# Batch 0 of a fused attention and gated FFN kernel: weight loads in 4 KB runs, conversion steps placed one by one, q turned by VectorE

## The chip, the cores and the metric

One core of a Trainium2 chip runs the whole program. The metric is the device time of one execution in microseconds; before the change it is 783.39 us, the median of three runs (782.16 to 783.68).

## What is computed

For each of 8 batches and 8 heads (S = 576 tokens, head size 64), 32 packed queries p attend to k and v, and then q attends to what came out, taken as keys and as values. The 4608 rows that result (8 heads side by side, 512 wide) go through a gated FFN. Cut to what matters:

```
pp  = softmax(p @ k.T / 8) @ v                  # per batch and head, 32 x 64
x   = softmax(q @ pp.T / 8) @ pp                # per batch and head, 576 x 64
x   = x.transpose(0, 2, 1, 3).reshape(4608, 512)
out = ((x @ w_a) * (x @ w_b)) @ w_out           # 512 x 1536, 512 x 1536, 1536 x 512
```

q, k, v and p are float32. The three weights come as float64, 6.29 MB each.

## The kernel before

**Stages of a batch.** Stage 1 (`stage1`, once for each half e of the heads) makes the scores of p against k, their softmax a1, its transpose and pp. Stage 2 (`stage2`, once for each half u of the tokens) makes the scores of q against pp and their softmax a2, which it stores as two float32r parts, `a2_hi` and `a2_lo`. x itself is never formed: `g_tiles` multiplies pp into a chunk c of the weights (128 columns of w_a and 128 of w_b for each of two f tiles), which gives `ghi` and `glo`, and `mm1` multiplies these by a2. So six chunks serve the twelve f tiles of a batch. An f tile of mm1 is two halves, one for w_a and one for w_b (`mm1_half`, 12 matmuls each, in a pair of PSUM banks of the pool `m`, of which there are two pairs). ScalarE copies the first half out, VectorE multiplies the second by it (both in `asb`), ScalarE rounds the product to `h_hi`, and GpSimd makes the rest `h_lo`. mm2 then adds up twelve f tiles against `wo` (hi and lo).

**Batch 0 and the weights.** The weights lie in DRAM as float64. Each piece of 512 KB is loaded raw into one of 12 buffers (`load_w`, `load_wout`) and turned to float32 by three steps: one on the high word (ScalarE, L170), one on the low word (ScalarE L176 or VectorE L173) and one that joins the words (VectorE, L178) into `w_ab`, or for w_out into `ob`, which is then split into `wo` hi (ScalarE) and lo (GpSimd). This happens once, while batch 0 runs; from batch 1 on the weights are in place. A chunk c needs four pieces: w_a and w_b, each for two pairs of heads. A piece of w_a or w_b is loaded by two DMAs, each to 64 of the 128 partitions, in runs of 2 KB. A piece of w_out is one DMA to 128 partitions, in runs of 4 KB.

**Order of the work.** It is written by hand; every engine takes its instructions in that order. `START` is the order of batch 0 up to the first f tile. In it K and Q are steps that turn k and q through TensorE (copies that bring two halves of the heads together, 18 transposes, copies out of PSUM), S0 and S1 begin stage 1, r0 and r1 go on with it, s0 and s1 are steps of stage 2, c is one round of up to three conversion steps, and g the first `g_tiles`. During mm1 and mm2 of a batch `between()` stands after every half f tile (slots 0 to 23) and after every f of mm2, and puts in what a table has for that slot: for batch 0 `PLAN_0`, which prepares batch 1 (Lp, Lk, Lv, Lq load; T0 turns p on TensorE; k0, k1, q0, q1 turn the two tiles of k or q on VectorE), and one round of conversions per slot. All loads go through SP's one DMA queue. At most eight DMAs are open; an issue beyond that waits for the eighth before it.

Of the kernel before, what the change touches and what calls it, by code (L numbers as in the profile page):

```python
# [19 lines left out]
def tile_packed_attn_gated_ffn(  # L20
# [144 lines left out]
    def to_f32(dst, raw, way):  # L165

        low, high = raw[..., 0], raw[..., 1].bitcast(F32)
        nc.scalar.activation(out=high, in_=high, func=AF.Prelu, scale=2.0 ** -112, alpha=-2.0 ** 32)  # L170
        yield
# [11 lines left out]
    def load_w(c, n):  # L183

        w, rr = (w_a, w_b)[n // 2], n % 2
        raw = wop.tile([P, 2, 2 * P, 2], U32, name="raw", tag="w")
        for e in range(E):
            row = (R * e + 2 * rr) * D
            nc.sync.dma_start(
                out=raw[D * e:D * e + D],  # L190
                in_=w.bitcast(U32)[row:row + 2 * D, 4 * P * c:4 * P * c + 4 * P].rearrange("(r d) f -> d r f", d=D))
        raws[c, n] = raw

    def load_wout(f):
# [3 lines left out]
        raws[NC, f] = raw  # L198

    wo_hi, wo_lo = [], []  # L200

    def convert(c, r):
        raw = raws.pop((c, r))
        if c < NC:
            i, rr = divmod(r, 2)
            yield from to_f32(lambda: w_ab[:, c, 2 * rr:2 * rr + 2, 2 * P * i:2 * P * i + 2 * P], raw, r == 3)
            return
        ts = []

        def dst():  # L210
            ts.append(sm.tile([P, DO], F32, name="ob", bufs=1))
            return ts[0]

        yield from to_f32(dst, raw, r % 3 == 2)
        t = ts[0]
# [15 lines left out]
    def stage1(b, e):  # L231

        rows = slice(64 * e, 64 * e + 64)
        s = bank_pair(True)
# [21 lines left out]
        tp, tq = bank(), bank()  # L256
# [19 lines left out]
    def stage2(b, u):  # L276

        TU = E * XH
        if b:
            hi, lo = (t[:, :, HS * u:HS * u + HS] for t in (a2_hi, a2_lo))  # L280
        else:
            hi, lo = (t.rearrange("p e (l x) -> p e x l", x=TX)[:, :, XH * u:XH * u + XH] for t in (a2_hi, a2_lo))
        x = bank_pair(True)
# [99 lines left out]
    def emit(b, plan, tasks={}):  # L383

        for name in plan.split():
            if name in tasks:
                next(tasks[name], None)
                continue
            what, e = name[:-1], int(name[-1])
# [52 lines left out]
    def converted(n):  # L442

        flight = []
        for _ in range(n):
            if not pieces:
                break
            if pieces[0] not in raws:
                load_pieces(1, True)
            flight.append(convert(*pieces.pop(0)))  # L450
            for c in flight[::-1]:
                next(c, None)
# [1 line left out]
            yield
            if len(flight) == 3:
                flight.pop(0)
        while flight:
            for c in flight[::-1]:
                next(c, None)
            yield  # L460
            if len(flight) == 1:
                drain(flight[0])
            flight.pop(0)
# [9 lines left out]
    q0 = scratch.tile([P, E, TX, D], F32, name="q0")
    for e in range(E):
        load_nat(k0[:, e].rearrange("p x d -> p (x d)"), k, 0, e)
    load_v(0, 0)
    for e in range(E):
        load_nat(q0[:, e].rearrange("p x d -> p (x d)"), q, 0, e)
    load_v(0, 1)
    load_pieces(8)  # L480
# [12 lines left out]
    for b in range(B):  # L493
        plan = dict(PLAN if b else PLAN_0)
        conv = converted(len(pieces))
        slot = [0]

        def between():
            emit(b + 1, plan.get(slot[0], "") if b + 1 < B else "")
            if b == 0:  # L500
# [13 lines left out]
        if b == 0:  # L514
# [57 lines left out]
```

## Time and profile before

| | |
|---|---|
| median of 3 runs | 783.39 us |
| the profiled execution's own time | 784.82 us |
| its span, first to last instruction | 783.0 us |
| TensorE matmul busy | 746.8 us (95%) |
| VectorE, ScalarE, GpSimd busy | 307.1, 288.1, 189.8 us |
| moved by DMA | 58.01 MB |
| mean granted TensorE clock | 0.974 |

The profiled execution took 784.82 us, of which 1.8 lie outside the span, and is 1.4 us above the median. The clock in the rows is a share of full speed, 1.00 or 0.50 in any short stretch; a mean over a longer stretch mixes the two. Times in rows are counted from the start of the span.

### The profile page before, as it was taken

How to read it: one execution, taken by the hardware profiler on the slowest of the kernel's cores; microseconds unless marked ns; L12 is line 12 of the kernel's file. 1: busy time of each engine (PE TensorE's matmuls, PEld its weight loads, DVE VectorE, ACT ScalarE, POOL GpSimd, SP SyncE). 2: the span in 40 equal slices, each digit the busy share in tenths (PEclk: the TensorE clock that was granted, in tenths of full speed). 3: DMA queues.
4: the chain of work that ended last, by engine and by line, in shares of the span. 5: the costliest groups of instructions: out<-in, count | busy, mean ns of one | idle time of the engine just before them, and what ended most of it. 6: DMA issues, size and time to landing. Idle time of an engine off the chain costs nothing.

```text
span 783.0 us, 13393 instructions
## 1 busy us (share of the span) xinstructions
PE 746.8 (95%) x5688; PEld 604.0 (77%) x5688; DVE 307.1 (39%) x487; ACT 288.1 (37%) x503; POOL 189.8 (24%) x146
## 2 busy tenths in 40 slices
PE   4667989999999999999999999999999999999998
PEld 2355677778887788788888788788877788888987
DVE  2756554555413445054421544144440444323200
ACT  2556774344312442144311443134411443134300
POOL 1012254323400234022410234012420224113300
PEclk8668999999999999999999999999999999999999
DMA  9999915145012340044201450142300410000001
GB/s 264 240 217 231 303 59 118 56 69 109 8 41 51 72 92 15 28 78 91 32 28 41 65 111 12 41 78 62 61 28 28 75 32 1 28 28 1 1 28 40
DMA packets 160459, 58.01 MB, mean 74 GB/s; under 512 B 139280, under 2 KB 147728, under 8 KB 160400
## 3 DMA queue, kind: packets, MB, share of 16 engines
q1 hardware_dynamic: 160400, 57.16, 31.4%
q8 instruction: 44, 0.72, 0.4%
q14 instruction: 15, 0.12, 0.1%
HBM read 47.71 MB, written 9.44 MB: 73 GB/s over the span
## 4 chain that ended last, share of the span: by engine, by line
PE 88%; DMA 4%; DVE 3%; ACT 2%; issue 1%; POOL 1%; SPq 0%; DVEq 0%; ACTq 0%; POOLq 0%
PE m L362 38%; PE m L340 38%; PE x L321 6%; PE s L237 2%; PE x L268 2%; DMA nat<-in_q_dram 1%; PE s L287 1%; DMA q<-in_q_dram 1%; PE x L258 1%; DMA raw<-in_moe_w_out_dram 1%; DMA raw<-in_moe_w_b_dram 1%; DVE w_ab L178 1%; POOL wo L83 0%; DVE ob L178 0%; ACT a_hi L309 0%
## 5 line engine op out<-in xcount | busy, mean ns | idle before, releaser
L362 PE MATMUL m<-wo,h_hi 128*128 128x512 f32 (+1 forms) x888 | 271.8, 388 | 3.2 <-ACT asb L348 2.0
L83 POOL TENSOR_TENSOR h_lo<-asb,h_hi 128x576 fp32r<-128x576 f32 x96 | 137.3, 1430 | 466.6 <-ACT h_hi L355 466.6
L362 PEld LDWEIGHTS m<-wo,h_hi 128*128 128x128 f32 x888 | 163.6, 189 | 47.6 <-ACT ob L375 7.5
L340 PE MATMUL m<-a_hi,ghi 128*128 128x288 f32 x768 | 175.5, 310 | 8.0 <-ACT a_hi L309 7.8
L362 PE MATMUL m<-wo,h_lo 128*128 128x512 f32 (+1 forms) x444 | 171.0, 385 | 0.0
L340 PE MATMUL m<-a_lo,ghi 128*128 128x288 f32 x768 | 164.9, 297 | 0.4 <-DVE a_lo L83 0.4
L340 PEld LDWEIGHTS m<-a_hi,ghi 128*128 128x128 f32 x768 | 122.7, 190 | 52.6 <-issue 37.6
L340 PE MATMUL m<-a_hi,glo 128*128 128x288 f32 x768 | 134.5, 297 | 0.0
L355 ACT CAST h_hi<-asb 128x576 fp32r<-128x576 f32 x96 | 64.8, 675 | 169.5 <-DVE asb L351 169.3
L340 PEld LDWEIGHTS m<-a_lo,ghi 128*128 128x128 f32 x768 | 125.6, 191 | 0.8 <-DVE a_lo L83 0.8
L351 DVE TENSOR_TENSOR asb<-m,asb 128x576 f32<-128x576 f32 x96 | 72.7, 757 | 131.9 <-PE m L340 124.6
L83 DVE TENSOR_TENSOR glo<-x,ghi 128x512 fp32r<-128x512 f32 x96 | 61.8, 685 | 141.5 <-ACT ghi L327 141.5
L340 PEld LDWEIGHTS m<-a_hi,glo 128*128 128x128 f32 x768 | 114.0, 191 | 0.0
L362 PEld LDWEIGHTS m<-wo,h_lo 128*128 128x128 f32 x444 | 83.9, 189 | 17.0
L375 ACT COPY ob<-m 128x512 f32<-128x512 f32 x35 | 20.6, 588 | 173.6 <-PE m L362 172.0
L348 ACT COPY asb<-m 128x576 f32<-128x576 f32 x96 | 61.5, 641 | 28.5 <-PE m L340 25.5
L321 PE MATMUL x<-w_ab,ppT 64*32 64x512 f32 x768 | 60.1, 615 | 7.5 <-DVE w_ab L178 7.5
L327 ACT CAST ghi<-x 128x512 fp32r<-128x512 f32 x96 | 51.3, 587 | 5.9 <-PE x L321 5.9
L118 DVE STREAM_TRANSPOSE xT<-nat 128x1152 f32<-128x1152 f32 x28 | 38.3, 1368 | 0.0
L321 PEld LDWEIGHTS x<-w_ab,ppT 64*32 64x32 f32 x768 | 9.5, 106 | 22.8 <-DVE w_ab L178 14.4
L170 ACT ACTIVATE raw<-raw 128x512 f32<-128x512 f32 x36 | 24.3, 677 | 3.0 <-DMA raw<-in_moe_w_out_dram 3.0
L298 ACT ACTIVATE t<-t 128x576 f32<-128x576 f32 x14 | 9.6, 687 | 42.8 <-POOL t L296 42.8
(91 smaller groups left out, 386.5 us busy)
## 6 DMA issues: line engine op xcount, KB each, us to landing
vt<-in_v_dram SPq DMA_DIRECT2D x16, 512.0 KB, 4.1
nat<-in_k_dram SPq DMA_DIRECT2D x56, 144.0 KB, 3.0
nat<-in_q_dram SPq DMA_DIRECT2D x56, 144.0 KB, 3.1
out_dram<-ob SPq DMA_DIRECT2D x31, 256.0 KB, 2.0
raw<-in_moe_w_a_dram SPq DMA_DIRECT2D x24, 256.0 KB, 8.7
raw<-in_moe_w_b_dram SPq DMA_DIRECT2D x24, 256.0 KB, 8.6
raw<-in_moe_w_out_dram SPq DMA_DIRECT2D x12, 512.0 KB, 6.7
out_dram<-ob SPq DMA_DIRECT2D x10, 128.0 KB, 2.3
```

The lines of the kernel that those rows point to most:

```text
L83: return eng.tensor_tensor(out=dst, in0=src, in1=hi.bitcast(F32), op=ALU.subtract)
L118: nc.vector.transpose(out=xT.rearrange("p r t -> p (r t)"), in_=t.rearrange("p r x d -> p (r x d)"))
L170: nc.scalar.activation(out=high, in_=high, func=AF.Prelu, scale=2.0 ** -112, alpha=-2.0 ** 32)
L237: nc.tensor.matmul(out=s[J * r:J * r + J, half, 0:HS], lhsT=pT[rows, r, :], rhs=xT_cols(b, "k", rows, r, half), start=True, stop=True)
L321: nc.tensor.matmul(out=gps[e][J * r:J * r + J, :], lhsT=ppT[rows, b % 2, r, :], rhs=w_ab[rows, c, r, :], start=True, stop=True)
L327: nc.scalar.copy(out=ghi[:, e], in_=gps[e])
L340: nc.tensor.matmul(out=ps[:, half, 0:HS], lhsT=gt[:, kt, i, :], rhs=at[:, kt, HS * half:HS * half + HS], start=(n == 0), stop=(n == len(st ...
L348: nc.scalar.copy(out=asb, in_=pa)
L351: nc.vector.tensor_tensor(out=asb, in0=pb, in1=asb, op=ALU.mult)
L355: nc.scalar.copy(out=hh, in_=flat)
L362: nc.tensor.matmul(out=o[:, cols], lhsT=ht[:, c0:c0 + P], rhs=wt[:, cols], start=(ft == 0 and n == 0), stop=(ft == NFT - 1 and n == 2))
L375: nc.scalar.copy(out=ob, in_=o)
```

## The change

It alters batch 0 alone, and the loads and conversions that run in it.

- A weight piece is now the 64 rows of one r for both halves of the heads and 512 float64 columns, so a run is 4 KB. It is still two DMAs to 64 partitions each. Eight pieces now serve two chunks at once (c = 0 and 1, then 2 and 3, then 4 and 5).
- The three conversion steps are letters of the tables, placed singly: A (high word, ScalarE), B (low word), C (join, VectorE) and D (split of w_out). B goes by `WAY`: of four pieces one to ScalarE, two to GpSimd, one to VectorE.
- q of batch 0 is loaded as in the other batches (eight DMAs in runs of 128 bytes) and turned by VectorE; its 18 transposes on TensorE and the copies around them go. The tokens of q then stand in their natural order, so a2 is written without a stride.
- The first loads come in another order (`FIRST`), and the loads for batch 1 stand elsewhere in `PLAN_0`.
- f tile 0 of batch 0 runs by halves of the tokens; stage 1 of e = 1 and stage 2 of u = 1 take their banks in batch 0 from the pool `m`.

The diff, cut to its core:

```diff
-                copy = nc.vector.tensor_copy if e else nc.gpsimd.tensor_copy if key == "q" else nc.scalar.copy
+                copy = nc.vector.tensor_copy if e else nc.scalar.copy
...
+    def low_word(raw, way):
+        low = raw[..., 0]
         if way:
-            nc.vector.tensor_scalar(
+            (nc.vector if way == 1 else nc.gpsimd).tensor_scalar(
                 out=low, in0=low, scalar1=2.0 ** -29, scalar2=7.0, op0=ALU.mult, op1=ALU.min)
...
-        w, rr = (w_a, w_b)[n // 2], n % 2
-        raw = wop.tile([P, 2, 2 * P, 2], U32, name="raw", tag="w")
+        w, r = (w_a, w_b)[n // R], n % R
+        raw = wop.tile([P, 4 * P, 2], U32, name="raw", tag="w")
         for e in range(E):
-            row = (R * e + 2 * rr) * D
+            row = (R * e + r) * D
             nc.sync.dma_start(
-                out=raw[D * e:D * e + D],
-                in_=w.bitcast(U32)[row:row + 2 * D, 4 * P * c:4 * P * c + 4 * P].rearrange("(r d) f -> d r f", d=D))
+                out=raw[D * e:D * e + D].rearrange("p f t -> p (f t)"),
+                in_=w.bitcast(U32)[row:row + D, 8 * P * c:8 * P * c + 8 * P])
...
+    WAY = (0, 2, 2, 1)
...
-        s = bank_pair(True)
+        s = bank_pair(b or e == 0)
...
+        if b == 0 and ft == 0:
+            pa, pb = (mm1_half(i, ghi, glo, halves=(0,)) for i in range(2))
+            mm1_half(0, ghi, glo, pa, (1,))
...
-    START = ("T0 K K K K Q K K K S0 Q S1 Q r0 r0 Q r1 Q r1 Q r0 Q c r1 P0 c c c s0 c s0 s1 s1 s0 c s0 s1 s1 g s0 s0 s1 s1 "
-             "c c c c")
+    FIRST = ("p0 k0 k1 w4 q0 v1 v0 q1 w8")
+    START = ("K K T0 B A K K K K K S0 A S1 C B A C r0 r0 r1 B C B r1 A A A r0 q0 r1 B A P0 q1 C s1 s1 A B s0 C C B "
+             "B s1 B B A s0 s1 s0 A A C C s0 g s0 B s1 s0 A A s1 A")
...
-    PLAN_0 = {0: "Lp0", 2: "Lk0", 4: "Lk1", 6: "Lv0", 8: "T0 k0", 9: "Lp2 k1 Lq0 Lq1", 15: "S0", 16: "r0",
-              19: "r0 S1", 20: "r0 r1 Lv1", 23: "r1", 24: "r1 Lv2", 25: "q0 P0", 26: "q1", 28: "Lk2", 29: "Lk3",
-              30: "s0", 31: "s0 s1", 32: "s0 s1", 33: "s0 s1", 34: "s1 s0 s0", 35: "s1", 36: "s1"}
-    NCONV = [1] * 24 + [1] * 12
+    PLAN_0 = ("B C C A | C C | B B A Lv0 B Lp0 B | Lk0 | A Lk1 C A C B B C C | B B C | B C A A B | T0 B | k0 A A C "
+              "A | C A B k1 | A C C B B A Lq1 Lq0 | B C | A C S0 |  |  | C D r0 A |  | C D | C D S1 | r0 | Lp2 B | "
+              "C r0 B r1 B | D A B A | Lv1 C B r1 B C | r1 D B | P0 Lv2 A | q0 C q1 B | A D C s0 A D D | A C s0 D "
+              "s1 A | D s0 Lk2 Lk3 |  | C s1 |  | s1 s1 | s0 D s0 s0 |  | C s1 s1")
```

**SP, the loads from the middle of the weights on, before.** `raw` is a weight piece, `nat` a tile of k (L109, first two) or q of batch 1, `vt` its v, `p_nat` its p:

```order
L189 DMA raw<-in_moe_w_b_dram 64x2x512 x4
L189 DMA raw<-in_moe_w_a_dram 64x2x512 x2
L133 DMA p_nat<-in_p_dram 128x2x64
L189 DMA raw<-in_moe_w_a_dram 64x2x512 x2
L189 DMA raw<-in_moe_w_b_dram 64x2x512 x2
L109 DMA nat_528<-in_k_dram 32x36x32 x4
L189 DMA raw<-in_moe_w_b_dram 64x2x512 x2
L189 DMA raw<-in_moe_w_a_dram 64x2x512 x2
L109 DMA nat_576<-in_k_dram 32x36x32 x4
L189 DMA raw<-in_moe_w_a_dram 64x2x512 x2
L189 DMA raw<-in_moe_w_b_dram 64x2x512 x2
L126 DMA vt<-in_v_dram 128x4x256
```

Now, from the first load of w_b:

```order
L194 DMA raw<-in_moe_w_b_dram 64x1024 x8
L194 DMA raw<-in_moe_w_a_dram 64x1024 x8
L194 DMA raw<-in_moe_w_b_dram 64x1024 x8
L194 DMA raw<-in_moe_w_a_dram 64x1024 x8
L194 DMA raw<-in_moe_w_b_dram 64x1024 x8
L127 DMA vt<-in_v_dram 128x4x256
L129 DMA vt<-in_v_dram 64x4x64
L134 DMA p_nat<-in_p_dram 128x2x64
L110 DMA nat_553<-in_k_dram 32x36x32 x4
L110 DMA nat_574<-in_k_dram 32x36x32 x4
L201 DMA raw<-in_moe_w_out_dram 128x1024 x10
```

Batch 1's p and k stood among the weight pieces and now stand behind all 24 of them.

**TensorE, around T0** (the matmul that reads `p_nat`), before, from the first half of f tile 3:

```order
L340 MATMUL m<-a_hi,ghi 128x288 x2
L340 MATMUL m<-a_lo,ghi 128x288 x2
L340 MATMUL m<-a_hi,glo 128x288 x4
L226 MATMUL x<-ident,p_nat 128x128
L340 MATMUL m<-a_hi,ghi 128x288 x2
L340 MATMUL m<-a_lo,ghi 128x288 x2
L340 MATMUL m<-a_hi,ghi 128x288 x2
L340 MATMUL m<-a_lo,ghi 128x288 x2
L340 MATMUL m<-a_hi,glo 128x288 x4
L321 MATMUL x<-w_ab,ppT 32x512 x8
```

Now:

```order
L335 MATMUL m<-a_hi,ghi 128x288 x2
L335 MATMUL m<-a_lo,ghi 128x288 x2
L335 MATMUL m<-a_hi,glo 128x288 x4
L220 MATMUL x<-ident,p_nat 128x128
L335 MATMUL m<-a_hi,ghi 128x288 x2
L335 MATMUL m<-a_lo,ghi 128x288 x2
L335 MATMUL m<-a_hi,ghi 128x288 x2
L335 MATMUL m<-a_lo,ghi 128x288 x2
L335 MATMUL m<-a_hi,glo 128x288 x4
L335 MATMUL m<-a_hi,ghi 128x288 x2
L335 MATMUL m<-a_lo,ghi 128x288 x2
```

T0 moved up by half an f tile (`PLAN_0` slot 8 to slot 7): it stood in f tile 4 and now stands ahead of it.

**VectorE, around T0's copy into `pT`**, before:

```order
L351 TENSOR_TENSOR asb<-m,asb 128x576
L178 SCALAR_TENSOR_TENSOR w_ab<-raw 128x2x256
L227 COPY pT<-x 128x128
L118 STREAM_TRANSPOSE xT_688<-nat_528 128x1152
L173 TENSOR_SCALAR raw<-raw 128x512
L178 SCALAR_TENSOR_TENSOR w_ab<-raw 128x2x256
L351 TENSOR_TENSOR asb<-m,asb 128x576
L118 STREAM_TRANSPOSE xT_713<-nat_576 128x1152
L178 SCALAR_TENSOR_TENSOR w_ab<-raw 128x2x256
L83 TENSOR_TENSOR glo<-x,ghi 128x512 x2
```

Now:

```order
L350 TENSOR_TENSOR asb<-m,asb 128x576
L221 COPY pT<-x 128x128
L119 STREAM_TRANSPOSE xT_688<-nat_553 128x1152
L182 SCALAR_TENSOR_TENSOR w_ab<-raw 128x2x256
L350 TENSOR_TENSOR asb<-m,asb 128x576
L182 SCALAR_TENSOR_TENSOR w_ab<-raw 128x2x256
L176 TENSOR_SCALAR raw<-raw 128x512
L119 STREAM_TRANSPOSE xT_717<-nat_574 128x1152
L84 TENSOR_TENSOR glo<-x,ghi 128x512 x2
L182 SCALAR_TENSOR_TENSOR w_ab<-raw 128x2x256 x2
L350 TENSOR_TENSOR asb<-m,asb 128x576
L182 SCALAR_TENSOR_TENSOR w_ab<-raw 128x2x256 x2
```

The order of the turns of k (L119) and of the multiplications `asb` behind them is much as it was, one f tile's multiplication behind each turn.

## Rows read from the trace of the kernel before

**Rows 1.** Stretches: us, length, busy of each engine (instructions), PEclk, DMA share, GB/s
```profile
5.00:10.00 5.00, 2.39 (x12) 2.42 (x13) 1.97 (x3) 1.92 (x4) 0.00 (x0) 1.00 1.04 355
10.00:15.00 5.00, 2.39 (x20) 1.61 (x22) 2.34 (x4) 0.76 (x2) 1.27 (x2) 0.95 1.09 283
15.00:40.00 25.00, 16.53 (x181) 7.38 (x173) 15.53 (x34) 13.12 (x25) 2.67 (x2) 0.64 1.07 240
75.00:80.00 5.00, 5.00 (x27) 4.05 (x20) 1.89 (x3) 1.78 (x4) 0.00 (x0) 0.56 1.05 295
80.00:85.00 5.00, 4.50 (x35) 4.04 (x38) 3.01 (x5) 3.98 (x7) 1.44 (x1) 1.00 0.98 156
90.00:95.00 5.00, 4.82 (x43) 3.72 (x41) 4.17 (x8) 3.73 (x9) 1.43 (x1) 1.00 1.02 411
...
200.00:300.00 100.00, 100.00 (x760) 82.33 (x758) 35.57 (x56) 32.17 (x56) 24.09 (x19) 1.00 0.23 50
```

**Rows 2.** TensorE's waits, the whole span: total us, times, longest
```profile
PE m L340 <- ACT a_hi L309: 7.8, 1, 7.8
PE x L321 <- DVE w_ab L178: 7.5, 10, 2.4
```

**Rows 3.** DMA from 214 to 226 us, GB/s in 40 slices, issues
```profile
GB/s 0 0 0 0 0 0 218 205 219 205 27 0 0 0 55 0 0 0 0 0 0 0 0 0 0 0 0 0 0 0 0 0 259 410 205 0 0 0 0 0
...
out_dram<-ob SPq DMA_DIRECT2D x2, 128.0 KB, 2.3
out_dram<-ob SPq DMA_DIRECT2D x1, 256.0 KB, 2.1
```

**Rows 4.** Timeline, VectorE and SP's DMA issues: start, us
```profile
6.71 1.41 DVE L144 COPY k_both<-k 128x576 f32<-128x576 f32 x2 [3.05 <-DMA k<-in_k_dram]
...
70.91 1.24 SPq L189 DMA_DIRECT2D raw<-in_moe_w_b_dram  x2
```

**Rows 5.** Timeline, TensorE in mm1 of batch 0
```profile
45.15 0.85 PE L340 MATMUL m<-a_hi,ghi 128*128 128x288 f32 x2 [7.77 <-ACT a_hi L309]
...
52.02 1.09 PE L321 MATMUL x<-w_ab,ppT 64*32 64x512 f32 x16
...
75.95 0.85 PE L340 MATMUL m<-a_hi,ghi 128*128 128x288 f32 x2
...
80.76 0.42 PE L340 MATMUL m<-a_hi,ghi 128*128 128x288 f32 x2
...
82.36 0.42 PE L340 MATMUL m<-a_hi,ghi 128*128 128x288 f32 x2
```

**Rows 6.** Timeline, TensorE from f tile 7 to the start of mm2
```profile
86.89 0.53 PE L340 MATMUL m<-a_hi,ghi 128*128 128x288 f32 x2
...
90.27 1.17 PE L237 MATMUL s<-xT,pT 64*32 64x288 f32 x16
...
113.41 1.14 PE L362 MATMUL m<-wo,h_hi 128*128 128x512 f32 x2 [2.04 <-ACT asb L348]
...
117.16 0.62 PE L362 MATMUL m<-wo,h_hi 128*128 128x512 f32 x2
```

**Rows 7.** Timeline, single steps of VectorE and GpSimd
```profile
10.76 1.27 POOL L144 COPY k<-q 128x576 f32<-128x576 f32 x2 [9.46 <-DMA q<-in_q_dram]
...
68.35 1.37 DVE L118 STREAM_TRANSPOSE xT<-nat 128x1152 f32<-128x1152 f32 x1
...
91.99 1.43 POOL L83 TENSOR_TENSOR h_lo<-asb,h_hi 128x576 fp32r<-128x576 f32 x1 [4.54 <-ACT h_hi L355]
...
92.41 1.55 DVE L178 SCALAR_TENSOR_TENSOR w_ab<-raw 128x512 uint32<-128x512 uint32 x1
...
95.19 0.75 DVE L351 TENSOR_TENSOR asb<-m,asb 128x576 f32<-128x576 f32 x1
95.86 0.68 DVE L178 SCALAR_TENSOR_TENSOR w_ab<-raw 128x512 uint32<-128x512 uint32 x1
...
98.33 1.29 DVE L83 TENSOR_TENSOR glo<-x,ghi 128x512 fp32r<-128x512 f32 x2 [1.79 <-ACT ghi L327]
```

More of the change, by code (lines that the diff above doesn't have):

```diff
@@ L197, in load_wout, with split_wout @@
             out=raw, in_=w_out.bitcast(U32)[P * f:P * f + P, :].rearrange("p (n t) -> p n t", t=2))
[L198 to L215, printed above, removed]
+        raws[NC2, f] = raw
+    WAY = (0, 2, 2, 1)
+    wo_hi, wo_lo, wo_f32 = [], [], []
+    def split_wout(t):
         wo = wop.tile([P, 2, DO], F32R, name="wo", tag="w")
@@ L255, in stage1 @@
         a1v = a1[:, 0:512].rearrange("p (t i) -> p i t", i=4)
-        tp, tq = bank(), bank()
+        if b == 0 and e:
+            pair = bank_pair()
+            tp, tq = pair[:, 0, :], pair[:, 1, :]
+        else:
+            tp, tq = bank(), bank()
         for i in range(4):
@@ L278, in stage2 @@
         TU = E * XH
[L279 to L283, printed above, removed]
+        hi, lo = (t[:, :, HS * u:HS * u + HS] for t in (a2_hi, a2_lo))
+        x = bank_pair(b or u == 0)
         for r in range(R):
@@ L307, in stage2 @@
         nc.vector.transpose(out=a2f.rearrange("p e t -> p (e t)"), in_=s2.rearrange("p x j -> p (x j)"))
-        a2v = a2f if b else a2f.rearrange("p e (x l) -> p e x l", l=TL)
-        nc.scalar.copy(out=hi, in_=a2v)
+        nc.scalar.copy(out=hi, in_=a2f)
         yield
-        lo_part(lo, a2v, hi)
+        lo_part(lo, a2f, hi)
         yield
     def g_tiles(b, c):
+        assert len(to_do["C"]) <= len(pieces) - 2 * R * (c // 2 + 1)
         gps = [bank() for _ in range(E)]
@@ L330, in g_tiles, with mm1_half @@
         return [(gv[0][:, u], gv[1][:, u]) for u in range(2)]
-    def mm1_half(i, ghi, glo):
-        ps = bank_pair()
+    def mm1_half(i, ghi, glo, ps=None, halves=range(2)):
+        ps = bank_pair() if ps is None else ps
         steps = [(gt, at, kt) for kt in range(E) for gt, at in ((ghi, a2_hi), (ghi, a2_lo))]
@@ L338, in mm1_half @@
         for n, (gt, at, kt) in enumerate(steps):
-            for half in range(2):
+            for half in halves:
                 nc.tensor.matmul(
@@ L342, in mm1_half @@
                     start=(n == 0), stop=(n == len(steps) - 1))
-        return ps[:, :, 0:HS]
+        return ps
     def mm1(b, ft, ghi, glo, between):
         asb = sm.tile([P, 2, HS], F32, name="asb")
-        pa = mm1_half(0, ghi, glo)
-        nc.scalar.copy(out=asb, in_=pa)
+        if b == 0 and ft == 0:
+            pa, pb = (mm1_half(i, ghi, glo, halves=(0,)) for i in range(2))
+            mm1_half(0, ghi, glo, pa, (1,))
+        else:
+            pa, pb = mm1_half(0, ghi, glo), None
+        nc.scalar.copy(out=asb, in_=pa[:, :, 0:HS])
         between()
-        pb = mm1_half(1, ghi, glo)
-        nc.vector.tensor_tensor(out=asb, in0=pb, in1=asb, op=ALU.mult)
+        pb = mm1_half(1, ghi, glo, pb, (1,) if pb is not None else range(2))
+        nc.vector.tensor_tensor(out=asb, in0=pb[:, :, 0:HS], in1=asb, op=ALU.mult)
         c0 = 64 * (b % 2)
@@ L440, in load_pieces, with convert @@
                     load_wout(r)
[L442 to L452, printed above, removed]
-            load_pieces(2)
[L454 to L463, printed above, removed]
+    def convert(x):
+        if x == "D":
+            if wo_f32:
+                split_wout(wo_f32.pop(0))
+                load_pieces(2)
+            return
+        if not to_do[x]:
+            return
+        c, n = to_do[x].pop(0)
+        if (c, n) not in raws:
+            load_pieces(1)
+        raw = raws[c, n]
+        if c < NC2:
+            raw = raw.rearrange("p (c f) t -> p c f t", c=2)
+        if x == "A":
+            high_word(raw)
+        elif x == "B":
+            low_word(raw, WAY[n % 4])
+        else:
+            assert len(to_do["A"]) <= len(to_do[x]) and len(to_do["B"]) <= len(to_do[x])
+            if c < NC2:
+                i, r = divmod(n, R)
+                both_words(w_ab[:, 2 * c:2 * c + 2, r, 2 * P * i:2 * P * i + 2 * P], raw)
+            else:
+                t = sm.tile([P, DO], F32, name="ob", bufs=1)
+                both_words(t, raw)
+                wo_f32.append(t)
+            del raws[c, n]
+            load_pieces(2)
     def first_g():
@@ L470, in tile_packed_attn_gated_ffn @@
     ep(tc.manual_schedule(engines={ET.PE, ET.DVE, ET.Activation, ET.Pool, ET.SP}))
-    load_p(0)
     k0 = scratch.tile([P, E, TX, D], F32, name="k0")
[L473 to L480, printed above, removed]
+    for name in FIRST.split():
+        what, i = name[0], int(name[1])
+        if what == "p":
+            load_p(0)
+        elif what == "k":
+            load_nat(k0[:, i].rearrange("p x d -> p (x d)"), k, 0, i)
+        elif what == "v":
+            load_v(0, i)
+        elif what == "q":
+            load(q, "q", 0, i)
+        else:
+            load_pieces(i)
     gfirst = []
-    tasks = {"K": turn_first("k", k0), "Q": turn_first("q", q0), "c": converted(8), "g": first_g()}
+    tasks = {"K": turn_first(k0), "g": first_g()}
     emit(0, START, tasks)
@@ L521, in tile_packed_attn_gated_ffn @@
                 between()
-            drain(conv)
+            for _ in pieces:
+                emit(0, "A B C D")
         for i, c0 in enumerate(tiles):
```

39 lines of the change are left out of this document (20 added, 19 removed).

## The prediction

> **What bounds the kernel now.** I read the stretches first. From 200 us on TensorE is busy without a break at full clock [rows 1], so a change to batch 0 can only win what batch 0 loses. Up to 100 us the DMA share is about 1: the queue never rests. From 15 to 40 us, when only weight pieces move, it brings 240 GB/s; from 90 to 95 us, only w_out, 411; from 80 to 85, only q in 128 byte runs, 156 [rows 1]. Then TensorE's own waits: 7.8 us for the first a2 and 7.5 in ten waits for `w_ab` [rows 2]. The timeline adds a loss that is no wait: after a pause on `w_ab` f tile 5 takes 4.81 us (75.95 to 80.76), while the next half takes 1.60 [rows 5]; the mean granted clock from 75 to 80 is 0.56 [rows 1], so TensorE ran mostly at the lower of its two levels, 1.2 GHz, which it had come down to while it waited. mm1 of batch 0 starts at 45.15 [rows 5], mm2 at 113.41 [rows 6]. I follow the change up to the start of mm2; behind it the same work follows at full clock, and a shift there is a shift of the end.
>
> **Do 4 KB runs load faster?** The pieces of w_out have 4 KB runs and move at 411 GB/s, so it seems so. But they also go to 128 partitions, the pieces of w_a and w_b to 64. The stores separate the two. Two stores of 64 rows, with 2 KB runs, move at 205 to 219 GB/s; a store of 128 rows, with the same 2 KB runs, reaches 410 [rows 3]. So half the partitions halve the rate and run length doesn't explain it. The changed load still writes 64 partitions per DMA. I take 240 GB/s for it, as now; the ends are 205 (the slowest slice of the 64 row stores) and 411 (w_out).
>
> The Trainium skill has the same cause (SBUF — State Buffer, "Door 1: The DMA port swizzle"): 64 partitions reach 8 of the 16 ports, at most about 218 GB/s. The rows say 240, and the measurement decides; by the page's figure the weights would take 5.4 us more and the forecast below would come out at 784.8, as an estimate.
>
> **When batch 1's p lands.** It now stands behind all 24 pieces and a v tile. k is in by 6.7 us (the copy that waited for it starts at 6.71 [rows 4]). Then 12.58 MB of pieces at 240 GB/s, 52.4; q of batch 0, 1.18 MB at 156, 7.6 (it took 3.3 at the 355 GB/s of its long runs [rows 1]: the new form costs 4.3); three loads of v, 0.59 MB each at 283 [rows 1], 6.3; p 0.3. Sum 73.3 us. The same sum for the kernel before puts its last piece of w_b at 76.6; its issue is at 70.91 [rows 4], behind a queue that was never empty, so the method is right to some 2 us.
>
> **The start.** The chain to the first a2 now waits for the second four pieces, since the first g needs eight, and exponentials of stage 2 stand on ScalarE behind the high words of those pieces. These land at 6.7 + 8 x 2.2 + 7.6 + 4.2, about 36 us; some ten us of steps (joins, softmax sums, two transposes, a2; TensorE waited 7.8 us for their tail before [rows 2]) give 46, against 45.15 now. That q's 18 transposes and its copies go saves nothing, for q's last tile lands at 27. The halves in f tile 0 can win no more than the 1 to 2 us until the second half of a2 is there. All of this is priced at nothing, and the cover is large: f tiles 0 to 3 take 12.8 us at full clock (3.2 each [rows 5]), 2.2 for two g (1.09 each [rows 5]) and some 3 for the slow clock, so f tile 3 ends at 64, and T0, next on TensorE, waits for p until 73.3. Only if the start slips by 9 us does it count.
>
> **From T0 to mm2.** TensorE: T0 at 73.3; f tile 4, slow for 5 us after this pause as after the one before 75.95, ends at 78.5; g 79.6; f tile 5 82.8; first half of f tile 6 84.4; S0 1.2 [rows 6], 85.6. VectorE beside it: k's tiles land at 77.1 and 80.9 (3.8 each at 156 GB/s). Turn 1.37, join 0.68, `asb` 0.75 [rows 7]: 79.9, in time for f tile 5's second half, whose bank it frees. Second turn 82.3, glo 1.29, two joins, `asb`: 85.7, again just in time for f tile 6's second half. That ends at 87.3; two joins 87.1; g, f tile 7 at 88.4. Before, f tile 7 began at 86.89 [rows 6] with S0 still to come, so here the change is 0.3 us late. What is left to mm2: five f tiles 16.0, g 1.1, S1 1.2, and three more groups of stage 1 (two of transposes, one for pp) at 0.9 each, taken below S0's 1.17 [rows 6] as they move fewer columns. That makes 21.0, and mm2 at 109.4. The kernel before took 26.5 from f tile 7, 25.3 without S0: it lost 4.3 to joins that came late for g and to the `asb` copy of 2.04 [rows 6]. After the change the joins of w_ab are done long before the last g, and ScalarE has fewer low words ahead of that copy. I let 1.0 of the 4.3 return: 110.4, 3.0 ahead. The slow start of mm2 (3.75 us for nine matmuls from 113.41 to 117.16 [rows 6], 1.6 more than the 2.1 that the 1.60 for twelve of 288 columns [rows 5] gives for nine of 512) goes if TensorE doesn't pause there; I take it whole: 4.6.
>
> **GpSimd's low words.** None is in the trace. 18 of 36 pieces get one; its length lies between 0.64 (a copy of 576 [rows 7]) and 1.43 (two operands [rows 7]), I take 1.0, nearer to the one-operand copy. Nobody waits for them where pieces wait for DMA. But a join took 1.55 instead of 0.68 when GpSimd was at work (91.99 and 92.41 [rows 7]). Two lie on the path at 87, so 0 to 1.7; I take 0.6, most of one. The sum is 4.0 us: 784.82 becomes 780.8, and of the median of 783.39, which is 1.4 lower, 779.4. In mm2 a piece of w_out needs at most 0.68 + 0.7 + 1.43 = 2.8 us (join, hi, lo) beside 2.8 of TensorE per f (twelve matmuls): covered, the more as ScalarE may run ahead.
>
> **The rivals.**
> - *Runs set the rate.* If 4 KB runs to 64 partitions move at 411, the pieces take 30.6, p lands at 51, T0 doesn't wait, the first f tile comes out at 38, and mm2 at 38.5 + 6.8 + 35.2 + 11 (five g, stage 1 of batch 1, T0) + 2 = 93.5. That is 20 us earlier: 763. For it: w_out. Against: the stores of 64 rows. 0.12.
> - *Slower by a queue on VectorE.* After the pause at T0, VectorE has k's two turns, six joins, glo and the multiplications that free the banks in one row with no slack. If all six joins meet GpSimd at 0.87 each, 5.2, and the late `asb` copy and slow start of mm2 stay (2.0 and 1.6, of which the latter is no loss against before), mm2 begins at 116.6: 3 us later, 786.5. It decides from mm2 at 115 on. The row at 92.41 speaks for it; that GpSimd has nothing to do in the pause speaks against. 0.22.
>
> The Trainium skill's rule for this (SBUF — State Buffer, "Who interferes with whom"): a VectorE instruction with two SBUF inputs waits for a GpSimd one that reads SBUF. The row at 92.41 agrees. By it every join that meets a low word is held, this rival's case.
> - *Even.* The weights come a little slower (225 GB/s adds 3.5), or half of the 4.3 returns and one collision more: within 0.2%. 0.16.
>
> **The numbers.** Forecast 0.50: 779.4, its own range 775 to 782 (below: p 2 us earlier and none of the 4.3 back; above: up to the even case). What a measurement of this kernel tells from no change is about 0.2%, 1.6 us. Faster is 0.50 + 0.12 = 0.62, same 0.16, slower 0.22. The range of 8 in 10 is 770 to 787: it takes in the slower rival, and leaves out 763.
>
> **What would show it.** Weight pieces at 240 GB/s in the stretch with nothing else; T0 waiting some 8 us for p, to about 73; f tile 7 at 88, mm2 at 109 to 111 and no wait there. A weight stretch near 400 GB/s, or T0 without a wait, would make the forecast wrong on the fast side; joins of 1.5 us in a row and `asb` as the releaser of mm1's waits after 80, on the slow side.

## The result: 0.35% slower, and the profile after

The changed kernel takes 785.07 us (median of 20 executions, 783.01 to 790.3), the kernel before 782.34 beside it (20 executions, 781.5 to 784.67). The ratio is 1.0035, 95% interval 1.0022 to 1.0048: 2.7 us slower, where 4.0 less was forecast. The profiled execution of the change took 783.26 us, one of its shortest, with a span of 781.5.

Stretches of the changed kernel (us, length, busy time of TensorE, its weight loads, VectorE, ScalarE and GpSimd with their instructions, PEclk, DMA share, GB/s), against [rows 1]:

```profile
35.00:40.00 5.00, 3.42 (x10) 0.44 (x12) 3.71 (x8) 2.60 (x6) 3.09 (x2) 0.50 1.04 241
...
70.00:75.00 5.00, 0.77 (x4) 0.80 (x5) 0.29 (x1) 0.05 (x1) 4.83 (x3) 0.55 1.15 175
...
85.00:90.00 5.00, 4.81 (x51) 2.99 (x51) 4.09 (x8) 4.05 (x9) 4.61 (x3) 1.00 1.03 417
...
115.00:120.00 5.00, 3.49 (x17) 2.58 (x16) 2.39 (x4) 1.19 (x2) 4.84 (x4) 1.00 0.38 117
```

The weight pieces move at 241 GB/s, as before, w_out at 417. From 70 to 75 TensorE is nearly idle, mostly at the lower clock (0.55): the pause at T0. New is the last row: GpSimd is full (4.84 of 5), ScalarE nearly idle, TensorE short of 1.5 us, and that inside mm2.

TensorE's waits over the whole span, against [rows 2] (total, times, longest):

```profile
PE x L220 <- DMA p_nat<-in_p_dram: 5.7, 1, 5.7
PE x L316 <- DVE w_ab L182: 5.7, 3, 3.3
PE m L335 <- ACT a_hi L303: 4.8, 1, 4.8
...
PE x L220 <- DVE pp L271: 2.0, 2, 1.5
...
PE m L361 <- ACT ob L374: 1.7, 2, 1.0
PE s L282 <- DVE xT L119: 0.7, 1, 0.7
```

The ten waits for `w_ab` are three now; T0 waits for p. The 2.04 us for `asb` ahead of mm2 [rows 6] are gone; pp and xT have taken their place, behind it.

TensorE's timeline, changed kernel, against [rows 5, 6]: first mm1, T0, f tile 7, the start of mm2, P0 (pp is turned on TensorE), the second half of S2 (the scores of stage 2, L282), and batch 1's first mm1:

```profile
47.19 0.61 PE L335 MATMUL m<-a_hi,ghi 128*128 128x288 f32 x1 [4.81 <-ACT a_hi L303]
...
74.23 0.45 PE L220 MATMUL x<-ident,p_nat 128*128 128x128 f32 x1 [5.74 <-DMA p_nat<-in_p_dram]
...
89.21 0.53 PE L335 MATMUL m<-a_hi,ghi 128*128 128x288 f32 x2
...
109.85 0.71 PE L361 MATMUL m<-wo,h_hi 128*128 128x512 f32 x2
...
118.13 0.33 PE L220 MATMUL x<-ident,pp 128*128 128x128 f32 x1 [1.51 <-DVE pp L271]
...
125.22 0.69 PE L282 MATMUL s<-xT,ppT 64*32 64x288 f32 x8 [0.68 <-DVE xT L119]
...
151.95 0.42 PE L335 MATMUL m<-a_hi,ghi 128*128 128x288 f32 x2
```

Up to mm2 this is the forecast: 47 for 46, 74.2 for 73.3, 89.2 for 88.4, 109.85 for 110.4, and mm2 begins without a wait. In the kernel before, mm2 began 3.56 us later [rows 6], but batch 1's first mm1 only 1.59 later:

```profile
153.54 0.42 PE L340 MATMUL m<-a_hi,ghi 128*128 128x288 f32 x2
```

So the stretch from mm2 to batch 1 took 42.1 us instead of 40.1. Behind it nothing differs: the own time less that start is 631.3 in both. What mm2 lost is to be read from VectorE and GpSimd, in the same trace (start, us, engine, line; in brackets the idle time ahead and what ended it):

```profile
112.48 0.88 DVE L176 TENSOR_SCALAR raw<-raw 128x512 uint32<-128x512 uint32 x1
117.19 0.69 DVE L182 SCALAR_TENSOR_TENSOR ob<-raw 128x512 uint32<-128x512 uint32 x1 [3.83 <-POOL wo L84]
117.80 0.28 DVE L271 TENSOR_SCALAR pp<-x,rs 128x64 f32<-128x64 f32 x1
...
118.71 1.37 DVE L119 STREAM_TRANSPOSE xT<-nat 128x1152 f32<-128x1152 f32 x1
123.18 0.69 DVE L182 SCALAR_TENSOR_TENSOR ob<-raw 128x512 uint32<-128x512 uint32 x1 [3.11 <-POOL wo L84]
123.79 1.37 DVE L119 STREAM_TRANSPOSE xT<-nat 128x1152 f32<-128x1152 f32 x1
...
111.92 2.49 POOL L176 TENSOR_SCALAR raw<-raw 128x512 uint32<-128x512 uint32 x1
114.50 1.42 POOL L84 TENSOR_TENSOR h_lo<-asb,h_hi 128x576 fp32r<-128x576 f32 x1
115.88 1.28 POOL L84 TENSOR_TENSOR wo<-ob,wo 128x512 fp32r<-128x512 f32 x1
117.24 4.54 POOL L176 TENSOR_SCALAR raw<-raw 128x512 uint32<-128x512 uint32 x2
121.86 1.29 POOL L84 TENSOR_TENSOR wo<-ob,wo 128x512 fp32r<-128x512 f32 x1
```

`ob` has one buffer. A join (L182) can't write it until GpSimd has taken the last piece's low part from it (`wo`, L84). GpSimd works in order, and ahead of that step stood a low word of 2.49 us and an `h_lo`, the next time two low words of 4.54. VectorE works in order too: behind the blocked join stood pp, which P0 waits for on TensorE, and the next time the turn of q, which S2 waits for. That is the theory A of the experiments.

### The profile page after: what moved, and what is told of

It is laid out like the page before. It is cut to its first block, busy times and chain, and to the rows that moved or that the text cites. A ratio compares the mean times of both kernels' runs of the same rounds, so it can differ in the third digit from the quotient of the medians.

```text
span 781.5 us, 13358 instructions
## 1 busy us (share of the span) xinstructions
PE 741.7 (95%) x5670; PEld 601.2 (77%) x5670; DVE 304.9 (39%) x483; ACT 276.2 (35%) x483; POOL 227.3 (29%) x162
## 4 chain that ended last, share of the span: by engine, by line
PE 82%; DMA 7%; SPq 4%; POOL 3%; DVE 2%; issue 1%; ACT 1%; POOLq 0%; DVEq 0%; ACTq 0%
PE m L335 37%; PE m L361 34%; PE x L316 5%; DMA raw<-in_moe_w_a_dram 3%; DMA raw<-in_moe_w_b_dram 3%; SPq L110 3%; PE s L231 2%; POOL wo L84 1%; PE x L266 1%; POOL raw L176 1%; PE s L282 1%; POOL h_lo L84 1%; PE x L256 1%; DVE ob L182 1%; SPq L194 1%
## 5 line engine op out<-in xcount | busy, mean ns | idle before, releaser
L84 POOL TENSOR_TENSOR h_lo<-asb,h_hi 128x576 fp32r<-128x576 f32 x96 | 138.0, 1438 | 441.3 <-ACT h_hi L354 440.8
L84 DVE TENSOR_TENSOR glo<-x,ghi 128x512 fp32r<-128x512 f32 x96 | 61.8, 686 | 133.9 <-ACT ghi L322 133.8
L176 POOL TENSOR_SCALAR raw<-raw 128x512 uint32<-128x512 uint32 x18 | 38.5, 2139 | 18.2 <-DMA raw<-in_moe_w_a_dram 13.8
L119 DVE STREAM_TRANSPOSE xT<-nat 128x1152 f32<-128x1152 f32 x30 | 41.1, 1370 | 3.3 <-DMA nat<-in_k_dram 1.7
```

Source lines behind the costliest of these rows:

```text
L84: return eng.tensor_tensor(out=dst, in0=src, in1=hi.bitcast(F32), op=ALU.subtract)
L119: nc.vector.transpose(out=xT.rearrange("p r t -> p (r t)"), in_=t.rearrange("p r x d -> p (r x d)"))
L176: (nc.vector if way == 1 else nc.gpsimd).tensor_scalar(out=low, in0=low, scalar1=2.0 ** -29, scalar2=7.0, op0=ALU.mult, op1=ALU.min)
```

## Experiments

Where a run starts from the changed kernel, its expectation says so. All times are medians. Three theories are tried: A, GpSimd's queue holds up the loop over w_out; B, the loss is the pause at T0; C, ScalarE is the bound of the loop.

**The w_out loop.** First, GpSimd loses the low words of w_out, and nothing else:

```
- low_word(raw, WAY[n % 4])
+ low_word(raw, WAY[n % 4] if c < NC2 else (0, 0, 0, 1)[n % 4])
```

> Edit to the changed kernel: the low words of the twelve w_out pieces leave GpSimd (ScalarE takes three of four, VectorE one); those of w_a and w_b stay there. Theory A, GpSimd's queue holds the w_out loop: with one ob buffer every join waits for GpSimd's last wo subtraction, that subtraction stood behind low words of 2.1 us, and behind the join on VectorE stood pp and q's turn. Then the waits of TensorE for pp (1.51 us) and xT (0.68, and half as much again in the two halves) and the longer wait for ob go: 3.4 us less, about 781.7, under the kernel before. Rival B, the loss is in the pause at T0 for p (5.7 us) and what follows it: no change within 1 us, about 785. Rival C, ScalarE becomes the bound of the loop in GpSimd's place (six more steps of 0.68): 1 to 3 us slower.

781.36 (779.74 to 784.11), 3.7 less, ratio to the kernel before 0.9979 (0.9968 to 0.999). In its trace GpSimd no longer holds up the joins for long (105 to 140 us, groups: busy, mean ns, idle ahead and its cause), and P0 and batch 1 come so:

```profile
L182 DVE SCALAR_TENSOR_TENSOR ob<-raw 128x512 uint32<-128x512 uint32 x9 | 6.2, 684 | 7.2 <-POOL wo L84 7.2
...
117.05 0.27 PE L220 MATMUL x<-ident,pp 128*128 128x128 f32 x1
...
149.00 0.43 PE L335 MATMUL m<-a_hi,ghi 128*128 128x288 f32 x2
```

In the changed kernel that group waited 14.1 us for GpSimd, here 7.2. mm2 starts at 110.44, so from there to batch 1 it is 38.56 us, 3.5 less than in the changed kernel. Of these, the waits for pp and xT are 2.2; S2, which the second of them cut in two, took 0.7 more there (2.1 for 1.4), and the waits for the copies into `ob` 0.5 more (1.7 for 1.2). Theory A holds, C falls.

Second, the other end of the same knot: two ob buffers, GpSimd keeps its low words. The edit below stands in three places, and `mx`, `sum2` and `nmx` get one buffer instead of two to make room:

```
- ob = sm.tile([P, DO], F32, name="ob", bufs=1)
+ ob = sm.tile([P, DO], F32, name="ob", bufs=2)
```

> Edit to the changed kernel: two ob buffers in place of one (mx, sum2 and nmx get one instead of two to make room); GpSimd keeps its low words. Theory A in its narrow form, that the single ob buffer ties VectorE's join to GpSimd's queue: pp and xT come on time, 2.5 to 3.5 us less, about 782. If GpSimd's throughput itself is short (its queue is 4.8 us busy of 5 from 115 to 120) TensorE waits for wo or h_lo instead, and the gain is under 1 us. Rival B (pause at T0): no change.

780.73 (780.02 to 781.4), 4.3 less, ratio 0.9968 (0.9956 to 0.998). The spread is 1.4 us in these five executions, against 7 in twenty of the changed kernel; ten executions of a further run with two buffers (the unbroken source below) have 4.0. VectorE writes pp 0.28 us after its product, and TensorE doesn't wait for it at P0:

```profile
115.50 0.28 DVE L271 TENSOR_SCALAR pp<-x,rs 128x64 f32<-128x64 f32 x1 [0.28 <-PE x L266]
...
118.22 0.27 PE L220 MATMUL x<-ident,pp 128*128 128x128 f32 x1
...
149.63 0.43 PE L335 MATMUL m<-a_hi,ghi 128*128 128x288 f32 x2
```

From mm2 (111.59) to batch 1 38.04 us, though GpSimd is as full as before (four low words, 2010 ns each). So not its throughput but the single buffer passes its delay on.

Is that knot new with the change? The same edit to the kernel before:

> Edit to the kernel before the change: two ob buffers (mx, sum2 and nmx get one). There GpSimd has no low words, and between two of its wo steps it has room for the h_lo of 1.43 us, so by theory A the single buffer costs little: a gain of at most 1.5 us, 781 to 783, while the changed kernel gained 4.3. Rival: the single buffer costs both kernels the same, 778.5, and then the rest of the change is worth nothing or a loss.

777.98 (777.91 to 778.56), ratio 0.9935 (0.9921 to 0.9948): the fastest version of all, and 5.0 less where at most 1.5 was expected. The rival of that run is right: the single buffer costs both kernels much alike (4.3 and 5.0), and with two the change still costs 2.75. In the kernel before, the knot sits ahead of mm2. A join waits for GpSimd, ScalarE's hi part of w_out waits for that join, the `asb` copy stands right behind it (112.72, 0.64 us), and mm2 follows at 113.41:

```profile
110.27 1.89 DVE L178 SCALAR_TENSOR_TENSOR ob<-raw 128x512 uint32<-128x512 uint32 x1 [1.40 <-POOL wo L83]
...
112.19 0.62 ACT L217 CAST wo<-ob 128x512 fp32r<-128x512 f32 x1 [1.46 <-DVE ob L178]
```

With two buffers the wait for `asb` is 0.21 instead of 2.04 [rows 6], mm2 begins at 108.78, and the slow start of mm2 goes with the wait: from there to batch 1 it is 38.19 instead of 40.1.

```profile
74.14 1.06 PE L321 MATMUL x<-w_ab,ppT 64*32 64x512 f32 x8 [2.35 <-DVE w_ab L178]
...
108.78 0.73 PE L362 MATMUL m<-wo,h_hi 128*128 128x512 f32 x2 [0.21 <-ACT asb L348]
...
146.97 0.43 PE L340 MATMUL m<-a_hi,ghi 128*128 128x288 f32 x2
```

**The queue up to p.** Where do those 2.75 lie? With two buffers mm2 begins at 108.78 without the change and at 111.59 with it. First p and k of batch 1 are taken out from behind the weights:

```
- "... s0 s1 s0 A A C C s0 g ..."            (START; PLAN_0 loses Lp0, Lk0 and Lk1)
+ "... s0 s1 s0 A A C Lp2 C Lk2 s0 g ..."    (and Lk1 in slot 0)
```

> Edit to the changed kernel: p and both k tiles of batch 1 are loaded among the last five pieces of w_b and w_a (behind the 19th, 20th and 22nd piece), not behind all 24. Theory B, the pause at T0 is what the change lost: T0 waits 0 to 1 us instead of 5.7 and f tile 4 runs at full clock (1.6 us): 4 to 7 us less, 778 to 781. Against it: the last piece lands near 80 instead of 71, so the g at 88 may wait; if that wait takes the place, no change within 1 us. Theory A: what is won at T0 is lost again in mm2, where GpSimd's loop ends last: less than 2 us, 783 or more.

786.69 (783.4 to 788.85), ratio 1.0041 (1.0025 to 1.0057): nothing won. T0 comes without a wait, and a new wait of 6.30 stands behind it:

```profile
68.12 0.27 PE L220 MATMUL x<-ident,p_nat 128*128 128x128 f32 x1
...
82.27 0.85 PE L335 MATMUL m<-a_hi,ghi 128*128 128x288 f32 x2 [6.30 <-ACT asb L347]
...
80.06 1.41 DVE L176 TENSOR_SCALAR raw<-raw 128x512 uint32<-128x512 uint32 x1 [6.76 <-DMA raw<-in_moe_w_b_dram]
```

The last pieces of w_b land later by what p and k take, and their steps stand ahead of the turn of k and of `asb` in the queues of VectorE and ScalarE. Whatever comes last in the queue of transfers is waited for. So this run moves the wait and doesn't decide theory B.

Then, with two ob buffers, q of batch 0 in long runs:

```
+ if b == 0 and key == "q":
+     for e in range(E):
+         nc.sync.dma_start(
+             out=t[64 * e:64 * e + 64].rearrange("p r x d -> p (r x d)"),
+             in_=src[b, R * e + 2 * i:R * e + 2 * i + 2].rearrange("r (l x) d -> (r l) (x d)", l=TL))
```

> Edit to the changed kernel with two ob buffers (780.7): q of batch 0 is loaded in runs of 4.6 KB (two DMAs of 64 partitions per tile) instead of runs of 128 bytes (four of 32); VectorE turns the tiles as before, so stage 2 of batch 0 gets q's elements in a wrong order. If the queue of transfers up to p of batch 1 is the bound of the front, the 3 to 4 us that q's short runs cost it come back: p lands near 70.5 and the time is 776.5 to 778, like the kernel before with two ob buffers (778.0). If not the queue but the order of the work on VectorE and ScalarE bounds the front, the time stays at 780 to 781.5.

778.26 (775.69 to 778.78), ratio 0.9931 (0.9904 to 0.9958): 2.5 less than with two ob buffers alone, and level with the kernel before with two. T0 is 3.40 us earlier than there (75.25), mm2 3.31 (111.59):

```profile
71.85 0.45 PE L227 MATMUL x<-ident,p_nat 128*128 128x128 f32 x1 [3.34 <-DMA p_nat<-in_p_dram]
...
108.28 0.71 PE L368 MATMUL m<-wo,h_hi 128*128 128x512 f32 x2
```

So q's load in short runs is the second cost, 2.5 us here, and it lies in the queue up to T0, so theory B is right in part. The run changes the length of the runs and with it the number of DMAs (four instead of eight) and doesn't tell the two apart. The 3.40 at T0 compares single traces: another trace with two ob buffers and q's short runs (the unbroken source below) has T0 at 73.85, 2.0 later than this one. Both costs taken away with the single buffer kept:

> Edit to the changed kernel, with its one ob buffer: the low words of w_out leave GpSimd (as in the run on that alone, 3.7 us) and q of batch 0 comes in long runs (2.5 us with two ob buffers; its elements so come in a wrong order). If the two costs lie in different places, they add: 785.1 - 3.7 - 2.5 = 778.9, and then what is left of the change (4 KB runs, steps placed singly, halves) wins nearly 4 us against the kernel before. If q's cost is only seen where GpSimd's loop is out of the way through the second ob buffer, or if the two hide each other, the sum falls short: 780 to 781.4.

779.83 (778.27 to 781.08), ratio 0.9955 (0.9943 to 0.9967): 5.2 of the 6.2, so they overlap by about 1 us. q's load is worth 1.5 beside the low words on ScalarE (781.36), and T0 comes only 0.75 earlier than in that run (74.47), mm2 1.41 (109.03):

```profile
73.72 0.45 PE L227 MATMUL x<-ident,p_nat 128*128 128x128 f32 x1 [7.65 <-DMA p_nat<-in_p_dram]
```

What is left of the change is then 3.3 us faster than the kernel before beside it (783.14); with two ob buffers it was worth 0 (778.26 and 777.98). So the rest may win just what the single buffer cost ahead of mm2 before (3.0 us: mm2 at 111.78 with one buffer, in the last trace of this section, and at 108.78 with two); no run shows it by itself.

**The rate of the weights.** Why 240 GB/s? Three tries. One DMA to 128 partitions per piece:

```
- for e in range(E):
-     nc.sync.dma_start(out=raw[D * e:D * e + D]..., in_=w.bitcast(U32)[row:row + D, ...])
+ nc.sync.dma_start(out=raw..., in_=w.bitcast(U32).rearrange("(e r d) f -> e r d f", e=E, r=R)[:, r, :, ...])
```

> Edit to the changed kernel: each piece of w_a and w_b is loaded by one DMA to 128 partitions instead of two to 64 each; bytes and runs (4 KB) as they are. If half the partitions are what halves the rate, a piece of 512 KB takes 1.28 us, as a piece of w_out, instead of 2.18: p of batch 1 lands 24 x 0.9 = 21 us earlier, near 53, T0 doesn't wait, the first a2 comes some 7 us earlier (eight pieces ahead of it), and conversions become the bound of mm1: 765 to 777. If something else sets the rate (the source's rows, the runs), the pieces stay at 240 GB/s and the time at 785.

973.26. It didn't test what it was meant to, since these DMAs used an eighth of the engines. A stretch of it:

```profile
95.00:100.00 5.00, 0.00 (x0) 0.00 (x0) 0.39 (x2) 0.39 (x1) 0.00 (x0) 0.50 0.13 52
```

A DMA share of 0.13 is 2 engines of 16, and the source's outermost step runs over the two e. The Trainium skill has it (DMA: Bandwidth & Descriptors, "Rules for kernel authors"): an outermost dimension smaller than 16 confines a DMA to at most that many engines. The trace agrees: 52 GB/s from two.

The halves on two queues, `(nc.scalar if e else nc.sync).dma_start`:

> Edit to the changed kernel: of each piece of w_a and w_b the second DMA (the other 64 partitions) is issued by ScalarE instead of SyncE, so both halves can move at once; bytes, runs and partitions of each DMA stay. If 64 partitions limit one DMA and the other half of the partitions is free meanwhile, the two together pass 240 GB/s, up to 411 while only weights move, and p of batch 1 lands up to 21 us before 74; the time then goes to 770 to 780. If the queues' engines are the limit whatever the partitions, the stretch from 20 to 70 us stays at 235 to 250 GB/s and the time at 785; ScalarE pays some 0.6 us per issue, 24 of them, so up to 5 us slower where it is on the path.

797.68 (795.79 to 799.84). ScalarE stood still at the start over its own issues, and TensorE behind it:

```profile
ACT L145 <- issue: 34.5, 1, 34.5
...
PE m L152 <- ACT both L145: 36.6, 1, 36.6
```

So its time says little of the rate. Its trace says more: from 32 to 44 us only pieces of w_a and w_b moved, on both queues, and the DMA engines were full (1.04) at 220 GB/s. The second queue added nothing to the 241 of one:

```profile
32.00:44.00 12.00, 6.53 (x51) 4.81 (x51) 3.14 (x7) 5.14 (x9) 0.00 (x0) 1.00 1.04 220
```

With two ob buffers as well:

> Edit to the changed kernel: the halves on two queues and two ob buffers together. If both are worth what they are alone and lie in different places (weights before 75 us, w_out behind 105), their gains add: about 4.3 less than the run with two queues alone. If the earlier weights only lead to the w_out loop sooner, with GpSimd's queue as the bound, the sum is 2 us or more short.

795.16 (792.98 to 795.84), 2.5 less than with the queues alone, not 4.3.

The source unbroken in memory, partitions and runs kept:

```
- in_=w.bitcast(U32)[row:row + D, 8 * P * c:8 * P * c + 8 * P])
+ in_=w_out.bitcast(U32)[row + 4 * P * c:row + 4 * P * c + D, :])
```

> Edit to the changed kernel with two ob buffers (780.7): the 48 DMAs of w_a and w_b read 64 whole rows of w_out, one unbroken 256 KB in memory, instead of 64 runs of 4 KB out of rows of 12 KB; partitions, bytes and runs are as they are (mm1 so computes with w_out's numbers). If the 64 partitions set the rate, 235 to 250 GB/s stay and so does 780 to 782. If the distance between the runs in memory sets it, the pieces move at up to 411 GB/s, p lands some 20 us before 74, T0 doesn't wait and the time is 765 to 775.

780.63 (778.37 to 782.38), the same as with two ob buffers alone; 50 to 65 us:

```profile
50.00:65.00 15.00, 14.81 (x98) 12.43 (x99) 9.53 (x16) 9.69 (x17) 6.78 (x4) 0.79 1.04 250
```

Neither run length nor the distance of the runs sets the rate: these DMAs read the same rows as the loads of w_out, at 250 GB/s, where those move at 417. What still differs is 64 partitions for 128, as read from [rows 3], and 256 KB in a DMA for 512. No run of this case loads a piece of w_a or w_b to 128 partitions with all engines, so the cause isn't shown.

**What the first traces were worth.** Another trace of the changed kernel:

> The changed kernel as it is, for another trace of it: executions lie between 783.0 and 790.3 and the first trace is of one of the shortest (783.26). If the spread arises in the w_out loop (theory A), a longer execution shows mm2 starting near 110 as before and longer waits for pp, xT, wo or h_lo between 110 and 150; if it arises at T0, mm2 starts later than 112 and the waits behind it are as in the first trace.

The profiled execution took 786.06 us (median 785.41). T0, mm2, batch 1:

```profile
75.72 0.45 PE L220 MATMUL x<-ident,p_nat 128*128 128x128 f32 x1 [7.50 <-DMA p_nat<-in_p_dram]
...
111.68 0.71 PE L361 MATMUL m<-wo,h_hi 128*128 128x512 f32 x2
...
154.80 0.42 PE L335 MATMUL m<-a_hi,ghi 128*128 128x288 f32 x2
```

Both happen: p lands 1.5 us later, and mm2 takes 43.1 instead of 42.1. The 1.0 more is the waits for the copies into `ob` (2.7 for 1.7); pp and xT are waited for as long as in the first trace. The median lies between the two traces. Three more traces of the kernel before:

> The kernel before the change as it is, for another trace of it: the first trace is of an execution of 784.82 us, while the timed ones have a median of 782.9. If the wait before mm2 (2.04 us for asb, mm2 at 113.4) is what made that execution long, this one begins mm2 near 111 and needs the same 39.7 us from there to the last product of batch 0; then the change, with mm2 at 109.9 and 111.7 in its two traces, wins little before mm2, and its loss of 2.5 us is what mm2 takes longer (41.6 and 42.6). If mm2 begins at 113.4 again, the change does win 2 to 3 us before mm2 and the loss must lie behind batch 0.

> The kernel before as it is, for a trace of an execution with a mean clock of 0.978 or more, as 58 of 63 have it (both traces so far are of the other kind, 0.974, and 784.8 and 785.7 us long). If the clock is what sets these two apart, this one is near 782.5, with f tile 5 (behind the pause on w_ab near 75) in 3.2 us instead of 4.8, mm2 begins near 111 to 112, and from there on it is as before.

> The same once more, for the case that the one ahead shows the lower clock again: as there.

The first two took 785.66 and 785.34 us at a mean clock of 0.974, with mm2 at 114.24 and 113.98. The third took 783.21 at 0.978:

```profile
51.29 1.09 PE L321 MATMUL x<-w_ab,ppT 64*32 64x512 f32 x16
...
73.36 1.21 PE L321 MATMUL x<-w_ab,ppT 64*32 64x512 f32 x8 [2.35 <-DVE w_ab L178]
...
111.78 1.22 PE L362 MATMUL m<-wo,h_hi 128*128 128x512 f32 x2 [2.05 <-ACT asb L348]
...
151.85 0.42 PE L340 MATMUL m<-a_hi,ghi 128*128 128x288 f32 x2
```

From mm2 to batch 1 it is 40.1 to 40.2 us in all four traces. The third reaches mm2 1.63 us earlier than the trace that the forecast stood on, and what differs is the granted clock, at two places. mm1 starts alike (45.21 and 45.15), but the clock rises earlier behind that wait (from 49 to 51 and from 51 to 53 us 0.68 and 1.00, against 0.50 and 0.73), and the next g comes at 51.29 instead of 52.02 [rows 5], 0.73 earlier. Behind the same wait of 2.35 for `w_ab` the clock falls in all four, in the third later: the eight matmuls after it take 1.21 there and 1.93 in the others, and mm2 follows 38.4 us behind their start instead of 39.3. f tile 5, for which 3.2 us was expected, still took 4.66. In the kernel before with two ob buffers the clock didn't fall there at all (1.00 from 70 to 82 us), and the eight took 1.06.

```profile
74.09 1.93 PE L321 MATMUL x<-w_ab,ppT 64*32 64x512 f32 x8 [2.35 <-DVE w_ab L178]
```

Of 75 timed executions of the kernel before, 5 have a mean clock of 0.976 or less (784.5 to 785.7 us) and 70 have 0.978 or more (781.1 to 784.3, median 782.8). Three of the four traced ones are of the rarer kind; why is not shown.

## Why the prediction was wrong

- **4 KB runs, 240 GB/s**: right, and the rival of 763 us falls with it (241 to 250 GB/s from 35 to 65 us, 229 to 239 in the second trace).
- **p lands at 73.3**: right (T0 at 74.23 and 75.72). The 4.3 us for q's short runs was in that sum; the traces with long runs have T0 earlier by 3.4 or 2.0 (two ob buffers) and by 0.75 (one), so that term looks too large, and the sum came out right in part by luck.
- **The start, T0 to mm2**: right in the sum. Forecast 110.4, or 111.0 with the 0.6 for collisions of joins, measured 109.85 and 111.68, and no slow start of mm2.
- **The step that failed**: "In mm2 a piece of w_out needs at most 0.68 + 0.7 + 1.43 = 2.8 us (join, hi, lo) ... covered". The three lengths were near what was measured (0.69, 0.62, 1.29; two of the nine joins from 105 to 140 us took 1.63), but they stand in queues: a join has to wait until GpSimd gets to the last piece's low part, with up to two low words ahead. Those were taken as 1.0 us, 1.43 at most, and take 2.14 on average (18 of them, 38.5 us). And the cost isn't that TensorE waits for w_out, which was what the step looked at: it waits for pp and xT, which stand behind the blocked join on VectorE. Forecast from mm2 to batch 1: 40.1 less the 1.6 of the slow start, 38.5. Measured: 42.1 and 43.1, so 3.6 to 4.6 of the error. Without GpSimd's low words in w_out it is 38.56, the forecast.
- **The base**: the gain was taken against a trace with mm2 at 113.41 and then subtracted whole from the median. That execution was one of the few with the lower mean clock; in the one trace of the usual kind mm2 begins at 111.78, so 1.6 us of the gain weren't there to win. The difference of 1.4 between the execution and the median was named in the forecast and its cause not asked for.
- Together 5.2 to 6.2 of the 6.7 us between forecast and result; the rest is within what two traces of the change differ by.
- **The slower rival** had the right kind of loss (work in order on VectorE behind joins that GpSimd holds up) in the wrong place. It put it behind the pause at T0, where the six joins took 0.64 to 0.68 us each. The argument against it was wrong too: GpSimd did have work in the pause (4.83 of 5 us from 70 to 75), but its low words were done at 75.4, and the first of these joins began at 78.04.
- **The even rival**: the wait for `asb`, half of the 4.3 us that it let return, didn't come back. Its slower weights (225 GB/s) show in part in the second trace (229 to 239, T0 at 75.72).
- **The knot in the kernel before** was read as "ScalarE has fewer low words ahead of that copy": the wait for `asb` came through the single ob buffer, as the run of the kernel before with two shows.

## What to carry to other kernels

A chain across engines with a single buffer isn't as long as the sum of its steps but as that sum plus everything queued ahead of each of them, and what it delays is whatever stands behind its blocked instruction: count both before calling a step covered, and try a second buffer first. When a gain is summed against one profiled execution, ask why that execution is longer or shorter than the median, and take out of the base what isn't in the usual one. A load in short runs is paid by whatever lands last in the same queue.

## What the runs showed of the hardware

- GpSimd's low word (uint32, multiply and min, 512 elements with 8 bytes from one to the next) takes 2.14 us on average, ScalarE's 0.68, VectorE's 0.42 alone and up to 1.53 beside GpSimd. The Trainium skill (GPSIMD Engine Reference, "Elementwise — side-by-side cycle accounting") has 769 ns as the best case for 512 elements in a tight loop. The low word, 512 elements too, takes nearly three times that here.
- Behind the same wait of 2.35 us on TensorE the granted clock falls sooner or later from one execution of a program to the next (1.93 or 1.21 us for the same eight matmuls), and in another program, with two ob buffers, it stayed at 1.00 (1.06 us).
- A DMA whose source has an outermost step of two used two of 16 engines (share 0.13, 52 GB/s).
